# Three stores of the second sequence change queue and place, and five unread products are dropped

## The chip, the cores and the metric

The kernel runs on one core of one Trainium2 chip. The metric is the device time of one execution in microseconds (us); the median of three runs stands for a kernel. The core has a matrix engine (TensorE, called PE in the profile; PEld is its weight load), VectorE (DVE), ScalarE (ACT), GpSimd (POOL) and SyncE (SP). Transfers between DRAM and on-chip memory are issued by SP, by POOL or by ACT and are carried by 16 DMA engines that all of these share; the profile calls what SP issues queue q1 and what POOL issues queue q0.

## The reference

```python
X = np.fft.rfft(x, axis=1)                       # x: 8 sequences x 3008 x 256
Yr = Xr @ w_r - Xi @ w_i + b_r
Yi = Xr @ w_i + Xi @ w_r + b_i
Y  = soft threshold of Yr, Yi with 0.01
y  = np.fft.irfft(Y, n=3008, axis=1)             # then reshaped to 24064 x 256
out = (sigmoid(y @ w_gate) * (y @ w_val)) @ w_out  # w_gate, w_val: 256 x 1536, w_out: 1536 x 256
```

Each sequence goes through a forward transform along its 3008 positions, a complex 256 x 256 product, a soft threshold and the inverse transform; every resulting row then goes through a gated feed-forward layer. The weights of that layer come in as 64-bit floats and are turned on the chip into pairs of rounded 32-bit halves.

## The kernel before

The transform of length 3008 is split as 47 x 64. A forward **a** step (`load_a`, `fwd_a`, `store_a`) takes one of 8 blocks of a sequence (`h` = 0 to 7), multiplies it by a 94 x 96 table and stores the 384 KB result to a DRAM buffer `zd[b]`. A **b** step loads `zd[b]` turned round, does the second part of the forward transform, the channel product and the first part of the inverse transform, and stores to `vd[b]`. An **inverse unit** (`load_v`, `inv_a`) loads 192 KB of `vd[b]`, does the last part of the inverse transform (8 matrix instructions on the tile `pia`) and yields 188 rows of the feed-forward layer's input. The layer takes 512 rows (a chunk `c`) at a time, in 12 steps `f`: `ffn1` (tiles `pg`, `pv`), then `ffn2` (`po`).

The core's program begins with sequence 0 (12 b steps, with preparations for sequence 1 and the weights' conversion beside them), then the a steps of sequence 1 that are left, then chunk 0 of the feed-forward layer. This opening lies in `tc.manual_schedule()` blocks: on each engine and each queue the instructions that are written there run in the order in which they are written. An engine that waits for something holds up what stands behind it on the same engine or queue. After chunk 0 the other sequences and the feed-forward layer are woven together.

The place of the change is the seam between these two manual blocks. The last a steps of sequence 1 (`h` = 5, 6, 7; `EARLY` = 4, `na` = 8) run at L925 to L929 in a loop `for h in range(EARLY + 1, na)`: `fwd_a(1, h)` gives PE work at L176 and copies on ACT and DVE at L177, then `store_a(1, h, nc.gpsimd)` issues the store at L187 on POOL. Step `h` = 4 has been stored on POOL before that. Then the buffers `p0` close and the second block begins: `load_v(u)` for the three units of chunk 0 (`own0` = 0, 1, 2; the load is issued on SP at L323 into the tile `vf`), `load_part()` (512 KB of raw feed-forward weights, SP, L807), `halves(3)` (three half a steps of sequence 2: `half_a`, PE L176 from the tile `xfh`, copied at L177 to `azh`, stored on POOL at L199, each followed by the load of a later half on SP, L191).

The first feed-forward unit (`unit(0)`) calls `inv_a` for units 0, 1 and 2. In the kernel before, five products of a weight tile by itself (`keep_warm`, L836, tile `warm`, which nothing reads) stand between `inv_a` of unit 0 and of unit 1. The first 512 rows need all three units: `inv_a` of the third ends with a copy on ACT (L332) and a subtraction on DVE (L333), and then `ffn1(0, 0)` starts at L399. Its weights' conversion (`from_f64`, DVE at L785, L787 and so on) and its gate product (DVE, L407) follow in order on DVE.

Of the kernel before, what the change touches and what calls it, by code (L numbers as in the profile page):

```python
# [27 lines left out]
FFT_BANKS, L1_BANKS, L2_BANKS = 3, 3, 2  # L28
# [5 lines left out]
LAST_GAP, SIDE_GAP = 20, 3  # L34
PRE = 2
WARM = 13
WARM_Z, WARM_V = 10, 5
EARLY = 4
AT_FIRST = 3
NCONV = 7  # L40
# [69 lines left out]
def tile_fft_mix_ffn(ctx: ExitStack, tc, x, w_r, w_i, b_r, b_i, w_one, w_out, mf, mi, mis, fa, fb, out):  # L110
    nc = tc.nc

    B, D, S = x.shape[0], w_r.shape[0], R1 * R2
    P = 128
# [26 lines left out]
    def bank(name, tag="fft", bufs=FFT_BANKS):  # L141
        return (psf if tag == "fft" else psl).tile([P, 512], F32, tag=tag, bufs=bufs, name=name)
# [43 lines left out]
    def store_a(b, h, queue=nc.sync):  # L186
        queue.dma_start(zv[b][:, 4 * h:4 * h + 4], held.pop(("x", b, h))[:2 * NQ])  # L187
# [131 lines left out]
    def load_v(u):  # L319
        own = 2 * UT <= u * UT < T0  # L320
        vf = p3.tile([P, 2, D], F32, tag="vo" if own else "vf", bufs=NVO if own else NVF, name="vf")[:2 * NQ]
        b, h = divmod(2 * u, H)
        nc.sync.dma_start(vf, vv[b][:, h:h + 2])  # L323
        held["v", u] = vf
# [10 lines left out]
    def inv_a(u):  # L335
        vf = held.pop(("v", u))
        pa = bank("pia")[:, :CT * UT].rearrange("p (c h k) -> p c h k", c=CT, h=2)
        for hh in range(2):
            for ct in range(CT):
                nc.tensor.matmul(pa[:, ct, hh], vf[:, hh, ct * P:(ct + 1) * P], fb_sb[:, :PT], start=True, stop=True)  # L340
        py = pa.rearrange("p c h k -> p c (h k)")
        lo = u * UT
        n = 0
        if lo < T0:
            c, at = divmod(lo, CW)
            n = min(UT, CW - at)
        if 0 < n < UT and lo + n < T0:
            t = p3.tile([P, CT, UT], F32, name="carry", bufs=1)[:, :, :UT - n]
            nc.scalar.copy(t, py[:, :, n:])
            held["carry", c + 1] = t, UT - n  # L350
        if n:
            split_y(c, at, n, py[:, :, :n])
        if lo + UT > T0:
            t = result("yf")
            t = t[:, :CT * (UT - n)].rearrange("p (c k) -> p c k", c=CT)
            nc.scalar.copy(t, py[:, :, n:])
            nc.sync.dma_start(yd[:, :, lo + n - T0:lo + UT - T0], t)
# [4 lines left out]
    def carry(c):  # L362
        if ("carry", c) in held:
            t, n = held.pop(("carry", c))
            split_y(c, 0, n, t)
# [55 lines left out]
    def ffn2(c, f):  # L421
        if f == 0:
            outs[c] = [bank("po", "l2", L2_BANKS) for _ in range(CT)]
        hh, hl = hts.pop((c, f))
        for ct, po in enumerate(outs[c]):
            wh, wl = (w2[:, f, v, ct * P:(ct + 1) * P] for v in range(2))
            nc.tensor.matmul(po, wh, hh, start=(f == 0), stop=False)
            nc.tensor.matmul(po, wl, hh, start=False, stop=False)
            nc.tensor.matmul(po, wh, hl, start=False, stop=(f == NF - 1))
        if (c, f) == (NPL - 1, NF - 1):  # L430
            last_outs.extend((po, out[ct * P:(ct + 1) * P, c * CW:(c + 1) * CW])
                             for ct, po in enumerate(outs.pop(c)))
        elif f == NF - 1:
            for ct, po in enumerate(outs.pop(c)):
                ot = result("ot")
                (nc.scalar.copy if ct == 0 else nc.vector.tensor_copy)(ot, po)
                nc.sync.dma_start(out[ct * P:(ct + 1) * P, c * CW:(c + 1) * CW], ot)
# [46 lines left out]
    def ffn_units():  # L484
        units, todo = [], {}
        seq = [(c, f) for c in range(NPL) for f in range(NF)]

        def own(c):

            return range(-(-c * CW // UT), -(-(c + 1) * CW // UT))  # L490

        for c in range(1, NPL):
            at = (c - 1) * NF
            for i, u in enumerate(own(c)):
                todo.setdefault(at + (0, 3, 6)[i], []).append(lambda u=u: load_v(u))
                todo.setdefault(at + (3, 6, 9)[i], []).append(lambda u=u: inv_a(u))
            todo.setdefault(at + 1, []).append(lambda c=c: carry(c))

        def unit(n):
            c, f = seq[n]  # L500
            if n == 0:
                for i, u in enumerate(own(0)):
                    if i == 1:
                        w = w1h[:, 0].rearrange("p i t n -> p (i t n)")
                        keep_warm(bank("warm", "l1", L1_BANKS), w[:, :P], w, WARM_V)
                    inv_a(u)
            ffn1(c, f)
            for t in todo.pop(n, ()):
                t()
            if n >= LAG and n - LAG < len(seq) - BEHIND:  # L510
                ffn2(*seq[n - LAG])
        return [lambda n=n: unit(n) for n in range(len(seq))], own(0), own(NPL - 1)[-1] + 1
# [233 lines left out]
    w1h = const.tile([P, NF, 2, CT, P], F32R, name="w1h")  # L746
# [86 lines left out]
    def keep_warm(o, l, r, n):  # L833

        for _ in range(n):
            nc.tensor.matmul(o, l, r, start=True, stop=True)  # L836
# [5 lines left out]
    ffn, own0, u0 = ffn_units()  # L842
    na = R1 // 8
# [15 lines left out]
    with tc.manual_schedule():  # L859
        for h in range(na):  # L860
            load_a(0, h)
        load_a(1, 0)
        for h in range(na):
            fwd_a(0, h)
            store_a(0, h)
            if h in (1, 3, 4):
                load_a(1, {1: 1, 3: 2, 4: 3}[h])
            if h == 2:
                load_mix()
        mfs[0] = load_mf(0)  # L870
        for q in range(2):
            load_b(0, q)
        mfs[1] = load_mf(1)
        load_bias4()
        load_part()
        mfs[2] = load_mf(2)
        for h in range(EARLY):
            fwd_a(1, h)
            if h == 1:
                wi_sb = mix_weights()  # L880
        keep_warm(bank("warm"), zero[:, :P], zero, WARM_Z)
        for q in range(NP + 2):
            if q + 2 < NP:
                load_b(0, q + 2)
            if 0 <= q - 1 < NP:
                mis_[q - 1] = load_mi(q - 1, True)
            if q < 2:
                for h in range(q * EARLY // 2, (q + 1) * EARLY // 2):
                    store_a(1, h)
            if q == 3:  # L890
                nc.sync.dma_start(fb_sb, fb)
                load_bias()
            if q % 2 and q <= NP:
                load_part()
            if q % 2 == 0 and 4 <= q < 4 + 2 * (na - EARLY):
                load_a(1, EARLY + q // 2 - 2)
            if q < NP:
                fwd_b(0, q, mfs[q], True)
            if q + 3 < NP:
                mfs[q + 3] = load_mf(q + 3)  # L900

            if q % 2:
                ops("sum word", 0)
                start_part(p0)
                ops("exp top", -1)
            elif q:
                ops("power mant", -1)
                if len(started) > 1:
                    ops("hi lo", 0)
                ops("one", -1)  # L910
            if q == 4:
                sub(bias_sb[:, 1], bias_sb[:, 1], bias_sb[:, 0])
            if 0 <= q - 1 < NP:
                mix4(0, q - 1)
            if q == NP + 1:

                fwd_a(1, EARLY)
                store_a(1, EARLY, nc.gpsimd)
            if 0 <= q - 2 < NP:
                inv_b(0, q - 2, mis_[q - 2], True)  # L920

        for bh in beside[:NR2K]:
            load_half(*bh)
        left = ["hi lo", "power mant one", "sum word", "hi lo"]
        for h in range(EARLY + 1, na):  # L925
            ops(left.pop(0), 0)
            fwd_a(1, h)
            store_a(1, h, nc.gpsimd)
        ops(left.pop(0), 0)  # L929
    p0s.close()  # L930
    p3 = p3s.enter_context(tc.tile_pool(name="p3", bufs=2, side="right", reuse_waits="tile"))
    with tc.manual_schedule():
        for u in own0:
            load_v(u)
        load_part()
        halves(AT_FIRST)
        for f in range(NF):
            ffn[f]()
            if parts:
                load_part()  # L940
            if f in (2, 3):
                tables[f - 2, 1] = load_mi(f - 2, False, later=True)
            if f in (5, 6):
                keep_mi(f - 5, tables[f - 5, 1])
            halves(AT_FIRST + (f + 1) * (len(beside) - AT_FIRST) // NF)
# [30 lines left out]
    n = len(a3) // 3  # L976
# [59 lines left out]
    with tc.manual_schedule():  # L1036
        for k in range(2 * NPR * NH):
            p, e = divmod(k, 2 * NH)
# [18 lines left out]
        n = NPR * NH  # L1057
# [36 lines left out]
```

## Time and profile before

| what | value |
|---|---|
| median of three runs | 2819.46 us (2818.62 to 2820.18) |
| the profiled execution | 2820.81 us, of which the span is 2819.0 us |
| PE busy | 2802.4 us, 99% of the span |
| DVE, ACT, POOL busy | 74%, 46%, 25% |
| granted TensorE clock, mean | 0.999 of full speed |

The times below are microseconds from the start of the span. A row of a timeline gives start, duration, engine, line of the kernel, operation, tile written and tile read, the count of instructions merged into the row, and in brackets how long the engine was idle just before and what ended that wait. Matrix instructions overlap, so that their ends are modelled.

### The profile page before, as it was taken

How to read it: one execution, taken by the hardware profiler on the slowest of the kernel's cores; microseconds unless marked ns; L12 is line 12 of the kernel's file. 1: busy time of each engine (PE TensorE's matmuls, PEld its weight loads, DVE VectorE, ACT ScalarE, POOL GpSimd, SP SyncE). 2: the span in 40 equal slices, each digit the busy share in tenths (PEclk: the TensorE clock that was granted, in tenths of full speed). 3: DMA queues.
4: the chain of work that ended last, by engine and by line, in shares of the span. 5: the costliest groups of instructions: out<-in, count | busy, mean ns of one | idle time of the engine just before them, and what ended most of it. 6: DMA issues, size and time to landing. Idle time of an engine off the chain costs nothing.

```text
span 2819.0 us, 38251 instructions
## 1 busy us (share of the span) xinstructions
PE 2802.4 (99%) x13896; PEld 2308.1 (82%) x13896; DVE 2082.3 (74%) x3109; ACT 1309.6 (46%) x2276; POOL 710.5 (25%) x638
## 2 busy tenths in 40 slices
PE   9999999999999999999999999999999999999999
PEld 6678888888899888888888888888888888888887
DVE  5777778667787536777777777777777777777776
ACT  4664544545455444444444444444444444444443
POOL 0211010224100002333333333333333343333321
PEclk9999999999999999999999999999999999999999
DMA  9866544666554661000000000000000000000000
GB/s 296 257 213 194 170 143 149 199 184 192 165 152 140 186 187 38 30 15 16 30 31 27 4 31 31 31 16 15 31 30 16 15 30 31 30 1 30 30 16 15
DMA packets 173469, 241.01 MB, mean 85 GB/s; under 512 B 14592, under 2 KB 124896, under 8 KB 173280
## 3 DMA queue, kind: packets, MB, share of 16 engines
q1 hardware_dynamic: 163776, 214.93, 24.8%
q0 software_dynamic: 9408, 23.60, 2.5%
q8 instruction: 110, 1.80, 0.3%
q14 instruction: 79, 0.65, 0.1%
q10 hardware_dynamic: 96, 0.04, 0.0%
HBM read 134.17 MB, written 104.33 MB: 85 GB/s over the span
## 4 chain that ended last, share of the span: by engine, by line
PE 94%; DVE 2%; DMA 2%; ACT 1%; issue 0%; SPq 0%; DVEq 0%; ACTq 0%
PE pd L659 11%; PE pa L659 11%; PE pc L659 11%; PE po L636 8%; PE po L635 8%; PE po L634 8%; PE pm L271 6%; PE pb L659 5%; PE pia L340 4%; PE pb L237 3%; PE pa L176 2%; PE pg L399 2%; PE pg L401 2%; PE pg L400 2%; PE pv L399 2%; PE pv L400 2%
## 5 line engine op out<-in xcount | busy, mean ns | idle before, releaser
L636 PE MATMUL po<-hl,w 128*128 128x512 f32 x912 | 362.5, 397 | 0.0
L635 PE MATMUL po<-hh,w 128*128 128x512 f32 x912 | 361.5, 396 | 0.0
L634 PE MATMUL po<-hh,w 128*128 128x512 f32 x912 | 360.8, 396 | 0.0
L718 POOL TENSOR_TENSOR c<-c,c 128x512 f32<-128x512 f32 x114 | 147.7, 1296 | 831.0 <-DVE c L714 640.1
L659 PE MATMUL pa<-a,w1h 128*128 128x512 f32 x912 | 284.0, 393 | 0.0
L659 PE MATMUL pc<-s,w1h 128*128 128x512 f32 x912 | 283.7, 392 | 0.0
L714 DVE TENSOR_TENSOR c<-u,pc 128x512 f32<-128x512 f32 x228 | 156.7, 687 | 114.7 <-PE pc L659 106.2
L689 DVE TENSOR_TENSOR u<-u,pb 128x512 f32<-128x512 f32 x228 | 155.3, 681 | 88.8 <-PE pb L659 62.6
L606 ACT CAST hh<-v 128x512 fp32r<-128x512 f32 x114 | 70.7, 620 | 306.2 <-DVE v L699 306.2
L636 PEld LDWEIGHTS po<-hl,w 128*128 128x128 f32 x912 | 171.5, 188 | 41.9
L634 PEld LDWEIGHTS po<-hh,w 128*128 128x128 f32 x912 | 172.0, 189 | 40.9
L635 PEld LDWEIGHTS po<-hh,w 128*128 128x128 f32 x912 | 171.0, 188 | 40.8
L659 PEld LDWEIGHTS pa<-a,w1h 128*128 128x128 f32 x912 | 171.2, 188 | 40.1
L659 PEld LDWEIGHTS pc<-s,w1h 128*128 128x128 f32 x912 | 171.0, 188 | 37.6
L610 POOL TENSOR_TENSOR hl<-c,hh 128x512 fp32r<-128x512 f32 x114 | 152.4, 1337 | 186.1 <-ACT hh L606 186.1
L271 PE MATMUL pm<-w_sb,xsh 128*128 128x256 f32 x1008 | 189.4, 288 | 1.4 <-ACT xf L177 1.1
L659 PE MATMUL pc<-s,w1l 128*128 128x512 f32 x456 | 177.5, 389 | 0.0
L659 PE MATMUL pa<-a,w1l 128*128 128x512 f32 x456 | 177.0, 388 | 0.0
L720 DVE TENSOR_TENSOR u<-u,pd 128x512 f32<-128x512 f32 x228 | 156.9, 688 | 24.5 <-DVE c L714 0.9
L693 DVE TENSOR_TENSOR v<-v,pc 128x512 f32<-128x512 f32 x228 | 156.6, 687 | 24.4 <-DVE v L691 0.5
L691 DVE TENSOR_TENSOR v<-u,pd 128x512 f32<-128x512 f32 x228 | 156.9, 688 | 24.0 <-DVE u L689 0.5
L685 ACT COPY u<-pa 128x512 f32<-128x512 f32 x228 | 133.7, 586 | 78.7 <-PE pa L659 78.6
(174 smaller groups left out, 6738.7 us busy)
## 6 DMA issues: line engine op xcount, KB each, us to landing
zf<-zd SPq DMA_DIRECT2D x96, 256.0 KB, 3.6
vf<-vd SPq DMA_DIRECT2D x128, 192.0 KB, 3.1
out_dram<-ot SPq DMA_DIRECT2D x93, 256.0 KB, 2.2
vd<-vz SPq DMA_DIRECT2D x84, 256.0 KB, 2.9
ypair<-yd SPq DMA_DIRECT2D x19, 1024.0 KB, 5.0
yd<-yf SPq DMA_DIRECT2D x103, 188.0 KB, 3.0
xf<-in_x_dram SPq DMA_DIRECT2D x48, 384.0 KB, 4.1
zd<-xf SPq DMA_DIRECT2D x44, 384.0 KB, 3.4
```

The lines of the kernel that those rows point to most:

```text
L271: nc.tensor.matmul(o, l, r, start=(i == 0), stop=(i == len(mms) - 1))
L610: sub_(hl, h, hh)
L634: nc.tensor.matmul(o, wh, hh, start=(f == 0), stop=False)
L635: nc.tensor.matmul(o, wl, hh, start=False, stop=False)
L636: nc.tensor.matmul(o, wh, hl, start=False, stop=(f == NF - 1))
L659: nc.tensor.matmul(o, l, r, start=not more and l is wh and r is xh, stop=l is wl, skip_group_check=more)
L689: add(u, u, b)
L691: add(v, u, d)
L693: add(v, v, c)
L714: add(c12, u, c)
L718: nc.gpsimd.tensor_mul(c12, g12, c12)
L720: add(u, u, d)
```

## The change

The five products between `inv_a` of units 0 and 1 go, with their constant `WARM_V`. The stores of blocks 5, 6 and 7 of sequence 1 leave POOL's queue, where each stood right behind its a step, and go to SP's queue, between the load of the second inverse unit (u = 1) and that of the third (u = 2).

```diff
-WARM_Z, WARM_V = 10, 5
+WARM_Z = 10
@@ in unit(n) of ffn_units
             if n == 0:
-                for i, u in enumerate(own(0)):
-                    if i == 1:
-                        w = w1h[:, 0].rearrange("p i t n -> p (i t n)")
-                        keep_warm(bank("warm", "l1", L1_BANKS), w[:, :P], w, WARM_V)
+                for u in own(0):
                     inv_a(u)
@@ end of the first manual block
         for h in range(EARLY + 1, na):
             ops(left.pop(0), 0)
             fwd_a(1, h)
-            store_a(1, h, nc.gpsimd)
         ops(left.pop(0), 0)
@@ start of the second manual block
-        for u in own0:
+        for i, u in enumerate(own0):
+            if i == 2:
+                for h in range(EARLY + 1, na):
+                    store_a(1, h)
             load_v(u)
         load_part()
         halves(AT_FIRST)
```

## Rows read from the trace of the kernel before

**Rows 1.** The page: busy time by engine; the chain's shares by engine.
```profile
PE 2802.4 (99%) x13896; PEld 2308.1 (82%) x13896; DVE 2082.3 (74%) x3109; ACT 1309.6 (46%) x2276; POOL 710.5 (25%) x638
...
PE 94%; DVE 2%; DMA 2%; ACT 1%; issue 0%; SPq 0%; DVEq 0%; ACTq 0%
```

**Rows 2.** Waits of PE from 106.7 to 2819: total, times, longest; the two longest.
```profile
PE pm L271 <- ACT xf L177: 1.1, 1, 1.1
PE pg L399 <- ACT yth L332: 0.6, 1, 0.6
```

**Rows 3.** Timeline of PE from 98 to 107.
```profile
98.49 2.74 PE L176 MATMUL pa<-xfh,fa_sb 94*96 94x512 f32 x6
101.18 1.10 PE L340 MATMUL pia<-fb_sb,vf 96*128 96x94 f32 x8
102.06 1.40 PE L836 MATMUL warm<-w1h 128*128 128x512 f32 x5
104.16 1.99 PE L340 MATMUL pia<-fb_sb,vf 96*128 96x94 f32 x16 [0.69 <-DMA vf<-vd]
106.78 0.54 PE L399 MATMUL pg<-yth,w1h 128*128 128x512 f32 x1 [0.62 <-ACT yth L332]
```

**Rows 4.** The chain that ended last, in order of time: start, us, what.
```profile
98.48 5.54 DMA vf<-vd
```

**Rows 5.** Timeline of SP's queue (issues, not transfers) from 98 to 101.
```profile
98.12 0.31 SPq L323 DMA_DIRECT2D vf<-vd  x1
...
98.48 0.61 SPq L323 DMA_DIRECT2D vf<-vd  x1
...
99.13 0.43 SPq L323 DMA_DIRECT2D vf<-vd  x1
99.61 1.04 SPq L807 DMA_DIRECT2D raw<-in_w_out_dram  x1
```

**Rows 6.** Issue to landing, us: loads 98.1 to 99.6; all loads; SP's stores after 130.
```profile
vf<-vd SPq DMA_DIRECT2D x3, 192.0 KB, 4.2
...
vf<-vd SPq DMA_DIRECT2D x128, 192.0 KB, 3.1
...
DMA to landing us min/median/max: 3.0/3.3/5.6
```

**Rows 7.** Timeline of POOL's issues from 96 to 102.
```profile
96.39 0.62 POOL L187 DMA_DIRECT2D zd<-xf  x1 [1.33 <-issue]
...
100.18 0.51 POOL L187 DMA_DIRECT2D zd<-xf  x1 [1.28 <-ACT w1h L792]
100.67 1.12 POOL L199 DMA_DIRECT2D zd<-azh  x2
```

**Rows 8.** Stretches: PE, PEld, DVE, ACT, POOL busy; PE clock, DMA share, GB/s.
```profile
22.00:28.00 6.00, 4.85 (x12) 1.46 (x10) 4.97 (x9) 3.63 (x7) 0.00 (x0) 1.00 1.02 385
...
99.10:102.00 2.90, 2.90 (x12) 1.34 (x11) 1.25 (x2) 2.30 (x4) 1.53 (x3) 1.00 0.88 259
102.00:104.00 2.00, 1.46 (x8) 0.90 (x7) 0.55 (x1) 0.47 (x1) 0.51 (x1) 1.00 1.04 320
104.00:107.10 3.10, 2.32 (x17) 2.05 (x17) 0.89 (x2) 1.01 (x3) 0.00 (x0) 1.00 1.02 402
107.10:110.50 3.40, 3.40 (x9) 2.57 (x9) 1.55 (x4) 2.71 (x4) 0.00 (x0) 0.50 1.06 337
```

**Rows 9.** POOL's queue, packets, MB and share: 102 to 104, then 104 to 107.
```profile
q0 software_dynamic: 9, 0.02, 5.5%
...
q0 software_dynamic: 211, 0.73, 60.0%
```

**Rows 10.** Timeline of DVE from 98 to 112.
```profile
98.98 0.68 DVE L177 COPY xf<-pa 96x512 f32<-96x512 f32 x1
...
107.11 0.42 DVE L785 TENSOR_SCALAR cv_e<-raw 128x512 uint32<-128x512 uint32 x1
...
111.65 0.69 DVE L407 TENSOR_TENSOR sg<-sg,pv 128x512 f32<-128x512 f32 x1 [2.18 <-PE pv L401]
```

## Prediction

> **What bounds the kernel now.** The page comes first: PE is busy 99% of the span and carries 94% of the chain that ended last [rows 1]. So the end moves when PE's work changes, when PE runs slower, or when PE stands idle. The list of PE's waits says where the last is still possible. From 106.7 us to the end it holds nine rows of which the longest is 1.1 us, and the second is the 0.6 us wait with which the first feed-forward product begins [rows 2]. From that product on, PE has nothing to wait for that is worth reading: whatever shifts its start shifts the end by as much, unless something new stalls it later. So I read PE's timeline around the seam [rows 3]. Three half steps run from 98.49 to about 101.2; unit 0's eight products start at 101.18 with no wait for its load; the five unread products start at 102.06 and are over at 103.46; PE then stands idle until 104.16, waiting for a load `vf`; units 1 and 2 run back to back (16 products, 1.99 us); and after another 0.62 us for the copy on ACT the feed-forward layer starts at 106.78. The chain names the load: issued at 98.48, landed 5.54 us later at 104.02 [rows 4]. In SP's timeline that is the second of the three, unit 1's [rows 5]. The third, issued at 99.13, landed at about 103.3 if the middle value 4.2 of the three is its own [rows 6], which fits with units 1 and 2 running without a gap. A load of this kind takes 3.1 us in the median of all 128 [rows 6], so unit 1's was held up by some 2.4 us. What held it up stands in POOL's timeline: stores of 384 KB issued at 96.39 and 100.18 (the first and the last of three; the second lies between) [rows 7].
>
> **The change part by part.**
>
> The five products are 1.40 us of PE time [rows 3], but they stand ahead of the wait for unit 1. While that load lands at 104.02 their removal is worth nothing; the time becomes idle time. It is worth up to 1.40 us only if unit 1's load is there by 102.06, and then only if unit 2's load isn't what PE waits for next.
>
> Units 0 and 1. Their loads are still the first on SP's queue behind the same wait, issued at 98.12 and 98.48. Without the three stores in their way I take the median 3.1 us [rows 6]: unit 1 lands at 101.6 instead of 104.02. Unit 0 starts at 101.18 as before, held by the half steps, and unit 1 follows at once. Both are over near 103.2 (two times 1.0 us of the 1.99 us for 16).
>
> Unit 2. Here is what the change adds. Three stores stand ahead of its load on SP's queue. The last of them has to wait for the copy of block 7 on DVE, which ends at 98.98 + 0.68 = 99.66 [rows 10]; an issue takes 0.3 to 0.45 us [rows 5], so unit 2's load is issued near 100.3, not 99.13. Queued behind that wait are this load, the raw weights and three loads for half steps; only the first is needed soon. Its transfer also stands behind 3 x 384 KB. The bytes up to and with unit 2 are 192 + 192 + 1152 + 192 = 1728 KB, or 1.77 MB. They start to flow about 1.0 us after the first issue (all of q1's transfers before begin near 99.1), and beside them POOL's three half-step stores (issued from 100.67 on [rows 7], 3 x 192 KB = 0.59 MB) take a part. How large a part is not in the trace of before, since SP's queue held no stores there. The bounds: POOL's queue moved 5.5% from 102 to 104 and 60% from 104 to 107 [rows 9]. The rate was 259 to 402 GB/s at the seam and 385 where loads and stores of sequence 0 filled the engines [rows 8]. I take half of POOL's 0.59 MB and 360 GB/s, between the 320 and the 402 that stand nearest: 2.07 MB / 0.36 = 5.75 us, from 99.1 to 104.85. Then some time passes until the landing is known: an undisturbed load takes 3.1 us, of which 1.0 is ahead of the data and 0.5 is data, so 1.6 us is left; in a full queue part of this is hidden, and I take 1.1. Unit 2 lands at 106.0. The lower end is 103.3, as before (the stores cost it nothing); the upper is all of POOL's bytes first at 320 GB/s and the whole 1.6 us: 99.1 + 2.36 / 0.32 + 1.6 = 108.1.
>
> From there: 0.14 us to the start as in the row of before (104.02 to 104.16), 1.0 us for eight products, 0.62 us for ACT's copy: the feed-forward layer starts at 107.75. Before it was 106.78. That is **+1.0 us**. The point at which the change breaks even is a landing at 105.0, which is 1.7 us behind where the load landed before.
>
> A rule against this change stands in the Trainium skill, "DMA: Bandwidth & Descriptors", section "Queues, rings and completion order": within a queue the descriptors of a DMA engine are consumed in ring order, and between queues the engine goes round in turn. By that rule the move lets unit 2 wait for all of the 1.18 MB, where before it took turns with them. The trace agrees in so far as POOL's share swings between 5.5% and 60% [rows 9] and unit 2 overtook the last POOL store; no run here yet shows the stores on SP's queue at this place. By ring order the sum is the one made here; by turns alone unit 2 would land as before, at 103.3, which is rival C.
>
> The clock. From 107.1 to 110.5 the granted clock was 0.50, the lower level of 1.2 GHz, and PE was busy all that time [rows 8]; before it fell, PE had been idle twice (0.69 and 0.62 us) and busy with the small products in between [rows 3]. The stretch costs about half of 3.4 us, 1.7 us. The change makes PE idler before: 1.40 us of products go, and the idle time ahead of unit 2 becomes 106.1 - 103.2 = 2.9 us. The trace has no such gap, so bounds: the clock could keep up if unit 2 comes early (-1.7 us); it could stay low for as long again (+1.7 us). I take +0.3, nearest to "the same stretch, begun a little earlier, so that unit 2's eight products are slow as well" (half of 1.0 us, in part).
>
> What costs nothing. POOL loses three issues; its half-step stores still wait for ACT's copies, so they go out as before. The DRAM reads of sequence 1's blocks wait for all eight stores; the last was issued at 100.18 on POOL [rows 7] and will be issued near 100 on SP, ahead of unit 2's load, so these reads aren't held up. The raw weights behind unit 2 land about 0.52 MB / 0.36 = 1.5 us after it, at 107.5. DVE first reads them at 107.11 in the profile of before, and by the new times near 108.0; then it has 2.18 us of idle time before the gate product [rows 10]. That covers it up to a landing near 110. If the cover is gone, each further microsecond delays PE by one.
>
> **Sum.** +1.0 + 0.3 = +1.3 us on the profiled execution, 2820.81 to 2822.1. That execution lies 1.35 us above the median of 2819.46, which is where the forecast is made: **2820.8 us**. About 0.2% (5.6 us) is what a measurement of this kernel can tell from no change, so this is "no change", on the slow side.
>
> **The rivals.**
>
> (B) The clock stays low longer. It is the same timeline as above, with the low stretch lasting up to 3.4 us more of busy time: +1.7 us, and with unit 2 at its upper end (+3.1 us) +4.8 us, 2824.3. For it speaks that the five products were work and idle time takes their place; against it, that they were over at 103.46 and the clock fell at 107.1 all the same. The Trainium skill, "TensorE: Matmul & The Clock Gate", section "Part 1: The HAM clock gate", says that the default state is throttled and that activity releases it; by that, less activity at the seam can only lengthen the stretch.
>
> (C) The stores cost unit 2 nothing, and the seam shrinks. Unit 2 lands by 103.3, its products end at 104.45 and the layer starts at 105.1: -1.7 us. If the clock then doesn't fall, another -1.7: 2816.1 to 2817.8. For it: unit 2 overtook unit 1 before, so a queue isn't strictly first come, first served, and 3.3 us is the median of SP's stores elsewhere [rows 6]. Against it: 1.18 MB at 385 GB/s is 3.1 us of full DMA engines.
>
> (D) Slower than before by more than 0.2%. The raw weights behind unit 2 land so late that DVE, standing at its first conversion, holds up the gate product, PE runs out of banks, and the weights that follow are late too. It decides from a landing near 110; to cost 5.6 us the first would have to land at about 116, or four of the ten that follow 1.4 us too late each. Against it: 0.52 MB behind unit 2 is 107.5, at the upper ends 109.6.
>
> (E) The order in which later work is woven in changes with this edit and happens to come out better by more than 5.6 us. PE's nine waits after the seam are all at or below 1.1 us [rows 2], so there is hardly that much to win.
>
> **How the numbers follow.** Forecast (unit 2 late by 2 to 4 us, result -0.5 to +3 us): 0.56. B (+3 to +5): 0.15. C (-3.5 to -0.5): 0.20. D: 0.05. E: 0.04. Faster by over 0.2%: E, 0.04. Slower: D, 0.05. Within 0.2%: the rest, 0.91. The range takes in the forecast, nearly all of C (down to 2816.3) and B up to +4.7 (2824.2), and leaves out D, E and the ends, under 2 in 10.
>
> **What would show it.** In PE's timeline after: units 0 and 1 as one row of 16 products from 101.2; then a wait for `vf` of 2 to 4 us; eight products; the layer's start at 107 to 109 (right), under 106 (C). In SP's: three stores between the loads, the third behind DVE's copy. In the stretches: the clock's low one of about the same length; longer is B. A wait of DVE for `raw` followed by a wait of PE at L399 would be D. The forecast is wrong if unit 2 lands before 105.0 or if PE shows new waits after 110.

## The result, and the profile after

The changed kernel takes 2827.26 us (median of 9 runs, 2826.83 to 2827.88), the kernel before 2819.59 us beside it (9 runs, 2818.29 to 2822.05). The ratio is 1.0027, 95% interval 1.0018 to 1.0036: **slower by 7.7 us, 0.27%**, where +1.3 us was forecast. The profiled execution has a span of 2825.6 us, 6.6 us more than that of before.

PE's timeline of the changed kernel answers to [rows 3].

```profile
99.53 2.74 PE L176 MATMUL pa<-xfh,fa_sb 94*96 94x512 f32 x6
102.11 1.92 PE L340 MATMUL pia<-fb_sb,vf 96*128 96x94 f32 x16
111.24 1.99 PE L340 MATMUL pia<-fb_sb,vf 96*128 96x94 f32 x8 [7.21 <-DMA vf<-vd]
113.85 0.79 PE L399 MATMUL pg<-yth,w1h 128*128 128x512 f32 x1 [0.62 <-ACT yth L332]
```

Units 0 and 1 run as one row, as forecast, and then PE waits 7.2 us for unit 2. Its eight products take 1.99 us where eight took 1.10 before, since the clock has fallen meanwhile (0.50 from 107.00 on). From unit 0's start to the layer's start is 11.74 us; in [rows 3] it is 106.78 - 101.18 = 5.60 us. The difference, 6.1 us, is nearly the whole of the span's 6.6. SP's timeline (issues) answers to [rows 5], and the chain to [rows 4]:

```profile
99.15 0.78 SPq L323 DMA_DIRECT2D vf<-vd  x2
100.05 1.91 SPq L187 DMA_DIRECT2D zd<-xf  x3
102.00 1.74 SPq L323 DMA_DIRECT2D vf<-vd  x1
103.80 1.80 SPq L804 DMA_DIRECT2D raw<-in_w_out_dram  x1
```

```profile
102.00 9.10 DMA vf<-vd
111.10 0.14 issue
```

The first two loads and the three stores are issued in under 3 us. The issue of unit 2's load itself takes 1.74 us, against 0.31 to 0.61 in [rows 5], and the load lands 9.10 us after its issue began. What the queues moved (packets, MB, share of the DMA engines), from 100 to 104 and then from 104 to 108, against [rows 9]:

```profile
q1 hardware_dynamic: 441, 1.18, 93.4%
...
q1 hardware_dynamic: 202, 0.59, 50.4%
q0 software_dynamic: 168, 0.54, 45.4%
```

From 100 to 104 SP's queue has the DMA engines to itself; from 104 on POOL's half-step stores take nearly equal turns and move 0.54 of their 0.59 MB there, ahead of the end of unit 2's load. The stretches answer to [rows 8] (PE, PEld, DVE, ACT, POOL busy; PE clock, DMA share, GB/s):

```profile
102.10:104.10 2.00, 1.93 (x17) 1.76 (x15) 0.42 (x1) 1.09 (x3) 1.09 (x3) 1.00 1.04 336
104.10:108.00 3.90, 0.00 (x0) 0.00 (x0) 0.68 (x2) 0.44 (x1) 0.00 (x0) 0.87 0.95 280
108.00:111.20 3.20, 0.00 (x0) 0.00 (x0) 0.00 (x0) 0.00 (x0) 0.00 (x0) 0.50 0.86 269
```

While PE waits, the DMA engines move 280 and 269 GB/s, not the 360 of the forecast and not the 402 of before while PE ran units 1 and 2. The clock is at its lower level (0.50) from 107.00 to 117.24, against 107.09 to 110.50 before. Of this the layer's products see 3.4 us, as much as before.

Each of these transfers lands in 16 parts, and PE starts 0.14 us after the last part of the load that it waits for (111.10 and 111.24). The trace holds the time of each part. For the transfers in flight here, and below them for two loads of the kernel before (first part, last part, us):

```
SP    unit 0      101.08  101.70
SP    unit 1      101.85  102.40
SP    block 5     102.79  104.46
SP    block 6     103.87  106.09
SP    block 7     104.83  107.47
POOL  half step   105.30  107.95
POOL  half step   105.83  108.78
POOL  half step   106.65  110.65
SP    unit 2      106.89  111.10
SP    raw         108.81  113.07
before:
SP    unit 1      102.06  104.02
SP    unit 2      102.64  104.39
```

The parts of units 0 and 1 land within 0.6 us of each other. Unit 2's are spread over 4.2 us, and its first part lands behind the first parts of all three half-step stores of POOL. The raw weights stand behind unit 2 in the queue, and yet their first part lands 2.3 us ahead of unit 2's last: the parts of one transfer do not keep step.

### The profile page after: what moved, and what is told of

It reads as the page before. It is cut to its first block, busy times and chain, and to the rows that moved or that the text cites. A ratio compares the mean times of both kernels' runs of the same rounds, so it can differ in the third digit from the quotient of the medians.

```text
span 2825.6 us, 38231 instructions
## 1 busy us (share of the span) xinstructions
PE 2802.0 (99%) x13891; PEld 2308.6 (82%) x13891; DVE 2080.9 (74%) x3109; ACT 1310.9 (46%) x2276; POOL 709.6 (25%) x635
## 4 chain that ended last, share of the span: by engine, by line
PE 95%; DVE 2%; DMA 2%; ACT 0%; issue 0%; SPq 0%; DVEq 0%; ACTq 0%
PE pd L656 11%; PE pa L656 11%; PE pc L656 11%; PE po L633 8%; PE po L632 8%; PE po L631 8%; PE pm L271 6%; PE pb L656 5%; PE pia L340 4%; PE pb L237 3%; PE pa L176 3%; PE pg L399 2%; PE pg L401 2%; PE pg L400 2%; PE pv L399 2%; PE po L427 2%
```

## The experiments

All 12 kernels ran beside the kernel before, whose median was 2819.6 to 2821.7 us in these sets. The tables and rows of one kernel are from one profiled execution. Theory **Q** says that unit 2's load is late by what stands ahead of it in the queues and that the end follows one to one; **K** that the missing products cost the time by the clock; **R** that later work is woven in a worse order; **T** that there is too much traffic at the seam in any order.

| kernel | unit 0's start | seam: from there to the layer's start | layer's start to the end of the span | median, us | ratio to before, 95% |
|---|---|---|---|---|---|
| before | 101.18 | 5.60 | 2712.2 | 2819.59 | |
| changed | 102.11 | 11.74 | 2711.7 | 2827.26 | 1.0018 to 1.0036 |
| e1 no products | 100.96 | 6.15 | 2712.4 | 2821.47 | 0.9998 to 1.0015 |
| e2 stores moved, products kept | 100.43 | 10.97 | 2712.0 | 2826.78 | 1.0013 to 1.0030 |
| e3 stores behind third load | 101.11 | 3.44 | 2719.0 | 2825.14 | 1.0009 to 1.0027 |
| e4 half-step stores on SP | 101.78 | 8.92 | 2713.9 | 2825.73 | 1.0009 to 1.0027 |
| e5 one store ahead | 101.82 | 4.32 | 2714.8 | 2823.76 | 1.0001 to 1.0019 |
| e6 two stores ahead | 101.58 | 8.92 | 2712.8 | 2823.86 | 1.0003 to 1.0021 |
| e12 two ahead, half steps on SP | 101.36 | 5.98 | 2713.2 | 2823.31 | 0.9997 to 1.0016 |
| e7 POOL, behind half steps | 101.35 | 3.44 | 2715.8 | 2823.89 | 1.0003 to 1.0021 |
| e8 ACT, behind half steps | 102.05 | 4.32 | 2716.0 | 2822.68 | 0.9998 to 1.0016 |
| e9 SP, behind half steps | 102.50 | 3.44 | 2712.3 | 2820.93 | 0.9993 to 1.0010 |
| e10 block 5 POOL, rest as e9 | 101.13 | 3.98 | 2713.5 | 2819.20 | 0.9984 to 1.0001 |
| e11 blocks 5, 6 POOL, rest as e9 | 100.77 | 5.31 | 2711.8 | 2822.45 | 0.9996 to 1.0013 |

The third and fourth columns carry the argument. Unit 0's start differs by up to 2 us between kernels whose instructions up to there are alike, so single spans are not finer than that, nor are the medians of neighbours in the table. The profiled execution of e11 is its fastest, 2819.62, 2.8 us under its median, so that its row does not show what its other executions lost.

**The two halves of the change, apart.** e1 is the kernel before without the products:

```diff
-                for i, u in enumerate(own(0)):
-                    if i == 1:
-                        ...
-                        keep_warm(bank("warm", "l1", L1_BANKS), w[:, :P], w, WARM_V)
+                for u in own(0):
                     inv_a(u)
```

> The kernel before without the five products; the stores stay on POOL. Theory Q (the load of unit 2 is late behind the stores in SP's queue, and the end follows it one to one): nothing of this is in here; PE's idle time ahead of units 1 and 2 grows from 0.7 to about 2.1 us, the feed-forward layer starts within 0.3 us of before, time within 1 us of before (2819.6). Theory K (the products kept the clock from staying low, and their loss is the cost): the low stretch gets longer than 3.4 us and the time rises by 2 us or more, toward 2827.

```profile
100.96 1.03 PE L340 MATMUL pia<-fb_sb,vf 96*128 96x94 f32 x8
103.55 2.94 PE L340 MATMUL pia<-fb_sb,vf 96*128 96x94 f32 x16 [1.56 <-DMA vf<-vd]
107.11 0.79 PE L399 MATMUL pg<-yth,w1h 128*128 128x512 f32 x1 [0.62 <-ACT yth L332]
```

The products' time becomes idle time, and the 16 products of units 1 and 2 take 2.94 us instead of 1.99, since the clock falls among them, at 104.38. The seam grows by 0.55 us; the median differs by 1.1 us from before, which the interval does not tell from nothing. e2 is the changed kernel with the products put back (the same lines, the other way round):

> The changed kernel with the five products put back; only the stores are moved. Theory Q: unit 2's load lands 7 us after unit 1 as in the changed kernel, PE waits some 6 us for it after the products, time 2826 to 2828. Theory K: the time comes back to within 3 us of before.

```profile
101.24 1.41 PE L836 MATMUL warm<-w1h 128*128 128x512 f32 x5
...
108.78 1.99 PE L340 MATMUL pia<-fb_sb,vf 96*128 96x94 f32 x8 [5.27 <-DMA vf<-vd]
```

With them the wait is still 5.27 us, the clock still falls (at 107.61), and the time is 2826.78. K falls; the move of the stores is the cost.

**How many stores stand ahead.** e3 puts all three behind the third load, e5 one ahead and two behind, e6 two ahead and one behind; the rest is as in the changed kernel. The edit of e5 is shown; in e6 `EARLY + 3` stands for `EARLY + 2`, and e3 has the second loop alone, from `EARLY + 1`.

```diff
         for i, u in enumerate(own0):
             if i == 2:
-                for h in range(EARLY + 1, na):
+                for h in range(EARLY + 1, EARLY + 2):
                     store_a(1, h)
             load_v(u)
+        for h in range(EARLY + 2, na):
+            store_a(1, h)
```

> The changed kernel with the three stores behind the third load on SP's queue instead of ahead of it. Theory Q: all three loads land by about 3 us after their issue, PE runs the three units without a gap, the feed-forward layer starts about 1.7 us earlier than before measured from the first unit; time 2815 to 2818.5. Theory K: the idle time is short, but the products are still missing: 2821 or more. Theory R (the later work is woven in another, worse order since the seam's instructions changed): 2824 or more, with PE's waits far behind the seam.

PE of e3, and the median time from issue to landing (us) of three half-step loads in it:

```profile
101.11 2.81 PE L340 MATMUL pia<-fb_sb,vf 96*128 96x94 f32 x24
...
114.09 1.99 PE L176 MATMUL pa<-xfh,fa_sb 94*96 94x512 f32 x2 [5.38 <-DMA xfh<-in_x_dram]
```

```profile
xfh<-in_x_dram SPq DMA_DIRECT2D x3, 192.0 KB, 9.4
```

The seam came out as Q said: no gap, and the layer starts 3.44 us after unit 0. The time did not. The raw weights and the half-step loads now stand behind the stores. The half-step loads take 9.4 us in the median, where three took 7.3 before and 7.0 in the changed kernel, and PE waits 5.38 us for one of them; the clock falls there (at 113.31). The lateness passed from one input to the next in the queue.

> The changed kernel with one of the three stores (block 5) ahead of the third load and two behind it. Theory Q, with the wait of 7.2 us as the price of 1.18 MB ahead: unit 2 waits a third or less, 0 to 2 us; but blocks 6 and 7 then stand ahead of the half-step loads, as in the run with all three behind the third load, and PE waits 3 to 5 us for such a load: 2823 to 2826. If only the bytes ahead of unit 2 count: 2819 to 2822.

```profile
104.42 1.10 PE L340 MATMUL pia<-fb_sb,vf 96*128 96x94 f32 x8 [0.68 <-DMA vf<-vd]
...
113.08 1.07 PE L176 MATMUL pa<-xfh,fa_sb 94*96 94x512 f32 x2 [1.23 <-DMA xfh<-in_x_dram]
```

The wait for unit 2 is in the range. That for a half step is 1.23 us, not 3 to 5, and 2823.76 us is in the range all the same. What POOL's queue had moved from 99 to 105, so up to the landing of unit 2 at 104.3:

```profile
q0 software_dynamic: 8, 0.03, 1.3%
```

> The changed kernel with two of the three stores (blocks 5 and 6) ahead of the third load, block 7 behind it. Price by bytes alone, in a line from 0.7 us of wait with one store to 7.2 us with three: PE waits 3 to 5 us for unit 2. If the wait for block 7's copy (it holds SP for about a microsecond) and the sharing with POOL's half-step stores make the jump, the wait is 1 to 3 us. Time 2823 to 2826 either way, since block 7 then stands ahead of the half-step loads.

```profile
107.89 1.99 PE L340 MATMUL pia<-fb_sb,vf 96*128 96x94 f32 x8 [4.39 <-DMA vf<-vd]
```

POOL's queue from 99 to 108, up to the landing of unit 2 in e6 at 107.75:

```profile
q0 software_dynamic: 183, 0.59, 23.3%
```

With one store ahead PE waits 0.68 us for unit 2, with two 4.39, with three 7.21. The 4.39 us lie in the range that was given for "bytes alone", not in the other, so e6 by itself does not tell the two apart. But the step from one to two is 0.39 MB, which at 300 GB/s is 1.3 us, and the wait grows by 3.7. In e5 unit 2 has landed when POOL's half-step stores begin to move; in e6 0.58 MB of them go ahead of its landing.

**POOL's half-step stores.** e4 is the changed kernel, e12 is e6, with the first three half-step stores on SP behind the raw weights:

```diff
-        nc.gpsimd.dma_start(zv[b][:, 2 * h:2 * h + 2], az)
+        (nc.sync if (b, h) in beside[:AT_FIRST] else nc.gpsimd).dma_start(zv[b][:, 2 * h:2 * h + 2], az)
```

> The changed kernel with the first three half-step stores (3 x 192 KB) moved from POOL's queue to SP's, behind unit 2's load and the raw weights. Theory Q with POOL's share as a main term: unit 2's load no longer has to share with 0.59 MB and lands 1.5 to 2.5 us earlier; time 2824.5 to 2826. If POOL's share hardly matters and the stores ahead in the queue do it all: 2827.

```profile
108.09 2.00 PE L340 MATMUL pia<-fb_sb,vf 96*128 96x94 f32 x8 [4.39 <-DMA vf<-vd]
...
vf<-vd SPq DMA_DIRECT2D x1, 192.0 KB, 6.8
```

> Two stores (blocks 5 and 6) ahead of the third load on SP, block 7 behind it, and the first three half-step stores on SP behind the raw weights instead of on POOL. If POOL's 0.59 MB going ahead is what makes the jump from 0.7 us of wait (one store ahead) to 4.4 us (two ahead): PE waits 1.5 to 2.7 us for unit 2. If the bytes in SP's own queue make it: 4 us or more, as with two ahead and the half-step stores on POOL. Block 7 and the half-step stores then stand ahead of the half-step loads, so the time can stay at 2822 to 2826 in both cases.

```profile
105.19 1.52 PE L340 MATMUL pia<-fb_sb,vf 96*128 96x94 f32 x8 [1.91 <-DMA vf<-vd]
```

Without POOL's share the wait is 4.39 us with three stores ahead (7.21 with it) and 1.91 with two (4.39 with it). So POOL's 0.59 MB, which none of the three units needs, costs 2.5 to 2.8 us of wait in either case, and the third store, with the wait ahead of its issue, 2.5 to 2.8 us. Without POOL's share the step from one store (e5) to two (e12) is 1.2 us, what 0.39 MB take at 320 GB/s. Of the 2.8 us that e4 gains at the seam 2.2 are lost behind the layer's start: the clock is low for 5.0 us of the layer instead of 3.4 (0.8 us), and PE's later idle time adds up to 1.3 us more, in waits far behind the seam; near it PE waits for no half step.

**Where the stores could go.** e7, e8 and e9 issue the three unit loads, the raw weights and the half steps first, then the stores, on POOL, ACT or SP. The edit of e7 is shown; e8 has `nc.scalar` in its place, e9 `nc.sync`.

```diff
+        for u in own0:
+            load_v(u)
         load_part()
         halves(AT_FIRST)
+        for h in range(EARLY + 1, na):
+            store_a(1, h, nc.gpsimd)
```

> All three loads first, then raw weights and half steps; the three stores stay on POOL's queue but behind the three half-step stores there. No products. Theory Q (what stands ahead in a queue sets when the next input lands): units 0 to 2 run without a gap, the layer starts 3.4 us after unit 0's start (5.6 in before), no load of a half step is late, since SP's queue holds no store; 2816 to 2818.5. Theory T (total traffic: the DMA engines have too much to move at the seam whatever the order): some input is late anyway and PE waits 3 us or more for it, 2820 to 2825.

PE of e7, and a row of SP's timeline in it:

```profile
123.72 1.48 PE L176 MATMUL pa<-xfh,fa_sb 94*96 94x512 f32 x2 [3.48 <-DMA xfh<-in_x_dram]
```

```profile
104.67 1.42 SPq L804 DMA_DIRECT2D raw<-in_w_one_dram  x1
113.54 0.39 SPq L229 DMA_DIRECT2D zf<-zd  x1
113.98 1.06 SPq L191 DMA_DIRECT2D xfh<-in_x_dram  x2
```

The seam is 3.44 us, but SP issues nothing from 106.1 to 113.5: next in its order is a read of the blocks that the stores write (`zf` from `zd`), and by the profile it waits 7.3 us for these stores. The half-step loads behind it come late, by 3.48 us for one; the median is 2823.89 us. That read isn't urgent: e9 issues it at 116.33, and PE waits for none of these reads there.

> As the run with the stores on POOL behind the half steps, but issued by ACT behind its three half-step copies. Theory Q: loads on SP's queue are as free as there; ACT's three issues (some 0.3 to 0.4 us each) delay its copies for the units by about 1 us; 2816.5 to 2820. Theory T: an input is late, 2820 to 2825.

```profile
106.37 0.49 PE L399 MATMUL pg<-yth,w1h 128*128 128x512 f32 x1 [1.24 <-ACT yth L332]
...
125.25 1.73 PE L176 MATMUL pa<-xfh,fa_sb 94*96 94x512 f32 x2 [1.85 <-DMA xfh<-in_x_dram]
```

The copies on ACT for the units end later (PE waits 1.24 us for them, not 0.62), and SP stands still for 7.6 us, by the profile for the stores, so that half-step loads are late again: both parts of the expectation in one run, 2822.68.

> The three stores on SP's queue, behind all three unit loads, the raw weights and the three half-step loads. Theory Q: nothing that is needed soon stands behind them any more (the next on SP waits for PE's unit 2 anyway); the layer starts 3.4 us after unit 0's start and PE doesn't wait for a half step; 2816 to 2819. If stores on SP's queue hold up everything after them by some 5 us (as the loads of the half steps in the run with the stores behind the third load), the raw weights and the next half-step loads are late instead: 2821 to 2825.

PE of e9, and below it a row of DVE:

```profile
102.50 2.81 PE L340 MATMUL pia<-fb_sb,vf 96*128 96x94 f32 x24
105.94 0.50 PE L399 MATMUL pg<-yth,w1h 128*128 128x512 f32 x1 [0.62 <-ACT yth L332]
...
117.88 0.50 PE L399 MATMUL pv<-yth,w1h 128*128 128x512 f32 x1 [1.02 <-ACT sg L405]
```

```profile
116.16 0.43 DVE L782 TENSOR_SCALAR cv_e<-raw 128x512 uint32<-128x512 uint32 x1 [1.66 <-DMA raw<-in_w_one_dram]
```

The seam is short, the clock stays at its upper level there, and all half-step loads come in time. What is late next is a part of the raw weights behind the stores: DVE waits 1.66 us for it, ACT for DVE, and PE 1.02 us for a bank that ACT has not read out. The median is 2820.93 us, not to be told from before, where 2816 to 2819 was expected. The profiled span is 0.8 us under that of before, with unit 0 starting 1.3 us later: in this execution the clock was low in the opening, from 34.84 to 38.26, where it stayed up in that of before.

e10 and e11 leave block 5, or blocks 5 and 6, on POOL as before and put the rest on SP as in e9. The edit of e10 is shown; e11 has `EARLY + 2` and `EARLY + 3`.

```diff
             fwd_a(1, h)
+            if h <= EARLY + 1:
+                store_a(1, h, nc.gpsimd)
@@ behind halves(AT_FIRST)
+        for h in range(EARLY + 2, na):
+            store_a(1, h)
```

> Block 5 stored on POOL at once, as in before; blocks 6 and 7 on SP behind the three unit loads, the raw weights and the half-step loads; no products. Theory Q: as the run with all three behind the half steps (no gap between the units, clock at its full level at the seam), and 0.39 MB less stands ahead of the raw weights that follow, so that PE's later 1.0 us wait for ACT goes: 2817.5 to 2820. If block 5 on POOL delays the unit loads again, a wait for vf of 1 to 2 us: 2820 to 2822.

```profile
101.13 1.99 PE L340 MATMUL pia<-fb_sb,vf 96*128 96x94 f32 x16
103.38 1.10 PE L340 MATMUL pia<-fb_sb,vf 96*128 96x94 f32 x8 [0.26 <-DMA vf<-vd]
```

> Blocks 5 and 6 stored on POOL at once, as in before; only block 7 on SP behind the unit loads, the raw weights and the half-step loads; no products. Block 6 is issued near the unit loads and shares with them: units 1 and 2 come up to 2 us later than with block 6 behind; 2818.5 to 2821.5.

```profile
100.77 1.03 PE L340 MATMUL pia<-fb_sb,vf 96*128 96x94 f32 x8
103.46 1.99 PE L340 MATMUL pia<-fb_sb,vf 96*128 96x94 f32 x16 [1.66 <-DMA vf<-vd]
```

With block 5 on POOL unit 2 is late by 0.26 us only, and e9's wait of 1.0 us is gone: 2819.20 us, the lowest median of all, 0.9993 of before (0.9984 to 1.0001), which is not clearly a gain. Not all went as expected. The clock fell at 105.93, just behind the layer's start, and of the 1.6 us that the seam is shorter than before, 1.3 are lost again later, in waits such as 0.32 us for a half step at 136.0 and 0.52 us for a copy on ACT at 169.8. In e11 block 6, issued at 98.08 on POOL, makes PE wait 1.66 us for unit 1, much as in e1 (1.56); its median, 2822.45 us, lies above the range. T falls: an order exists, e9 and e10, in which the same bytes hold up hardly anything. R falls as well: in the changed kernel the last column of the table, 2711.7 us, is no longer than before.

## Why the prediction was wrong

**What held.** The end follows the layer's start: the last column of the table stays at 2711.7 to 2712.4 us for before, changed, e1, e2 and e11, while the seam goes from 5.3 to 11.7. Removing the products is worth nothing by itself. Units 0 and 1 run together, and unit 2's load becomes what PE waits for. Its issue came 2.85 us after unit 0's load (102.00 - 99.15); 2.2 was forecast. The wait ahead of block 7's store was 0.4 us and, by the profile, for a copy on ACT (`azh`) and not for DVE's copy, which ended at 100.70.

**The step that failed** is the landing of unit 2: 106.0 was forecast, 4.8 us after unit 0's start, and even the upper end, 108.1, is 6.9 us after it. It was 111.10, 9.0 us after unit 0's start at 102.11. The mechanism was the forecast's own; two terms of that sum were mis-sized, and the clock's term behind it.

- POOL's half-step stores. I counted half of 0.59 MB, 0.8 us. They cost 2.5 to 2.8 us (e4 against the changed kernel, e12 against e6). It is a matter of timing: unit 2's load, issued late, falls just into the time in which they move; with one store ahead (e5) it does not.
- The rate and the tail. The 360 GB/s came from stretches with the loads on SP and the stores on POOL, the tail of 1.1 us from an undisturbed load. With no POOL stores in the way (e4) the seam is still 8.92 us, where the sum without their 0.8 us gives 5.8; 1.0 us of that is the clock's, so some 2.2 us belong to rate, tail and the long issue. The trace of the changed kernel shows both at work. From 100 to 108 the two queues moved 2.31 MB, 289 GB/s, which took 8.0 us where 5.75 us had been forecast for 2.07 MB. By then q1 had moved 1.77 MB, as many bytes as stood in it up to and with unit 2; unit 2 landed 3.1 us later, where 1.1 was forecast, since its 16 parts were spread over 4.2 us and some of the raw weights had gone ahead of the slow ones. Why some parts are so much slower than others, and why the rate was lower, stays open.
- The clock. I took +0.3 us. Unit 2's eight products ran wholly at the lower level (1.99 us, where the sum had 1.0), which is +1.0; the layer's own stretch at that level was as long as before.

The seam adds up: forecast 106.78 - 101.18 + 1.0 = 6.6 us, measured 11.7; 4.2 of the difference come from the landing, 1.0 from unit 2's clock. The median's 7.7 us is 1.1 more than the span's 6.6, since the profiled execution of before, 2820.81, lies 1.2 us above its median; and 0.9 of the span's is in the opening ahead of unit 0. Unit 0's start scatters by 2 us over the kernels, so this part is not shown to belong to the change.

**A reading that was wrong.** The 4.2 us of [rows 6] is not the third load's own: it is the middle of the two landings that the view could tell, 2.92 and 5.54 us. By its parts, unit 2 landed at 104.39 before, 5.3 us after its issue and 0.4 behind unit 1. So it had overtaken neither unit 1 nor the last POOL store, which was issued 1.05 us after it. The lower end of the forecast and rival (C) began at 103.3 where 104.4 was measured; with that (C) would have gained 0.6 us and not 1.7, and the point of breaking even lay 0.6 us behind the old landing and not 1.7.

**The rivals.** (B) was right in kind and small. (C), which had 0.20, did not occur: with three stores ahead of it unit 2's load landed behind all three; a seam shorter than before is e3's. What spoke for (C) was the reading above. (D) had the right sign with the wrong mechanism: PE never waited for the raw weights in the changed kernel; in e9 that chain (DVE waits for `raw`, ACT for DVE, PE for ACT) appears and costs 1.0 us. (E) did not occur. What was missing among them is the forecast's own mechanism at two and a half times its size (7.2 us of idle time ahead of unit 2, where 2.9 was forecast). Its upper end had all of POOL's bytes, but 320 GB/s and a tail of 1.6 us, where 289 GB/s and 3.1 us were measured: these bounds came from stretches in which stores and loads did not stand in this order on two queues at once. The Trainium skill, "DMA: Bandwidth & Descriptors", section "Queues, rings and completion order", has within a queue ring order and between queues turns. Both show here: from none to three stores ahead, PE's wait for unit 2 goes 0, 0.7, 4.4, 7.2 us, and 0.59 and 0.54 MB were moved side by side from 104 to 108. By that rule the unit's load waits for the 1.18 MB ahead of it and for as much again of the other queue as there is; the forecast had half of the second part.

## What to carry to other kernels

Ahead of a load that the bounding engine waits for, count everything that its queue still holds and everything that another queue will move in the meantime, all of it and not a share, and then ask for the slowest of the 16 parts and not for the mean. Check that a median over a few loads includes the one that you read it for. If stores are moved out of one input's way, look which input stands next behind them: here the lateness went from unit 1 to unit 2, then to the half steps (e3), then to the raw weights (e9), and an order paid only in so far as the next input had slack. Work that nobody reads costs nothing while the engine would wait anyway, and then its removal is worth nothing either (e1).

## What the runs showed that was not expected

The issue of unit 2's load on SP takes longer the more stores stand ahead of it: 0.42 us with one (e5), 0.74 and 1.23 with two (e12, e6), 1.71 and 1.74 with three (e4, the changed kernel), against 0.31 to 0.61 in [rows 5]. So the stores also delay the time at which what follows gets into the queue; what holds the issue up is not shown. The parts of one 192 KB load, landing within 0.6 us when nothing stood ahead of it, were spread over 4.2 us behind three stores beside POOL's stores.

The clock is the other surprise. In the four kernels in which PE runs the three units without a gap (e3, e7, e8, e9) it stays at its upper level past the layer's start. In the ten others, down to e10 with its gap of 0.26 us, it falls between 104.4 and 107.6, ahead of the layer's start or up to 0.8 us behind it. The length of the last gap does not decide when: after 1.56 us (e1) the 16 products of units 1 and 2 took 2.94 us, after 1.66 us (e11) 1.99. So in these traces a gap at the seam came with a fall of the clock, and could cost more than its own length; the runs do not vary the gap alone.
